# Both score passes of an attention block contract over 128 rows

## The chip, the cores and the metric

The kernel runs on one core of one Trainium2 chip. The metric is the time of one execution on the device in microseconds (us), the median of several executions; lower is better. TensorE (PE) does the matrix products, with its weight loads shown as a row of their own (PEld); VectorE (DVE), ScalarE (ACT) and GpSimd (POOL) do the elementwise work; DMAs are issued from the queue of SyncE (SP).

## The reference

Inputs are q, k and v of 8 batches, 8 heads, 576 tokens and 64 features, and a feed-forward with weights 512 x 2048 and 2048 x 512 whose activation is a quotient of polynomials. In short:

```python
scores = scale * np.matmul(q, k.transpose(0, 1, 3, 2))     # scale = 1/sqrt(64)
mask = block_i >= block_j                                  # blocks of 64 tokens
scores = np.where(mask, scores, -1000000000.0)
attn = softmax(scores)                                     # over the keys
x = (attn @ v) as [4608 tokens, 512 features]
h = x @ w_in
g = (a[0] + a[1]*h + a[2]*h2 + a[3]*h3) / (1 + |b[0]|*|h| + |b[1]|*h2 + 1e-6)
out = g @ w_out                                            # float32
```

## The kernel before

Every operand of a product is held as two numbers, a high part that the matrix engine multiplies exactly and a low remainder, and a product is the sum of the parts that matter: hi·hi, hi·lo and lo·hi.

**Attention.** Work goes by pairs of heads, 32 pairs in all. For a pair, `prep` transposes q and k so that features lie on the partitions (head 0 on rows 0 to 63, head 1 on rows 64 to 127), and splits them: ACT writes the high part (L357), DVE the remainder (L358). q hi, q lo and k hi go into the tile `hl`, k lo into a tile `kl`. Then two DMAs for each head build the tile `kq` (L365, L366): its first slot has q hi on the head's own 64 partitions and q lo on the other 64, its second slot has k hi on both halves. Three `kq` buffers serve the two heads of a pair and the first head of the next one.

`scores` takes the queries of a head in five blocks (t = 0 to 4; 64, 128, 128, 128 and 128 queries, against 64, 192, 320, 448 and 576 keys; the last in two pieces of 288). That makes 12 pieces for a pair and 384 in all. A piece has two passes into one bank of PSUM: L412 contracts over 128 rows (q hi and q lo with k hi), L413 over the head's own 64 rows (q hi with k lo, read from `kl`). Where the piece ends in the diagonal block (256 of the 384), a third matmul in bf16 adds the mask (L416). DVE takes the maximum of the bank (L417), ACT the exponential (L429), POOL multiplies by the reciprocal of the sum (L438, L442).

`transp` transposes the probabilities on PE (L463) and splits them into `pt1` (queries 0 to 319) or `pt2` (320 to 575), high part by ACT (L466), remainder by DVE (L467). Block 0 of the keys is the first 64 keys of both heads, side by side. `pv` multiplies with v, which lies in `vpad` between columns of zeros so that both heads of a pair come out of one product (L479), and stores x to DRAM (L484).

**Feed-forward.** It runs in two phases over d_ff: phase A (10 of 16 blocks) is woven into the attention from its second batch on, phase B follows alone. A unit of work is two blocks of d_ff for 256 tokens: `first` (24 matmuls, L201), the activation on ACT, POOL and DVE, `split` (L233, L234), and `second` (12 matmuls, L250). During the first batches DVE, ACT and POOL also split the float64 weights (L121 to L148).

**What sets the order.** The program emits attention step by step with lags: exponentials one step after the scores, transposes some ten steps after; feed-forward steps by a schedule in step numbers. The framework then reorders the instructions with its own model of time and fixes the order on each engine; at run time each engine takes its instructions in that order, and a waiting DMA on the SP queue holds those behind it.

Of the kernel before, what the change touches and what calls it, by code (L numbers as in the profile page):

```python
# [9 lines left out]
F32 = mybir.dt.float32  # L10
F32R = mybir.dt.float32r
# [12 lines left out]
CT = 256                 # tokens of a feed-forward chunk  # L24
# [35 lines left out]
def attn_ffn_kernel(  # L60
# [21 lines left out]
    # x^T, hi and lo (row = feature of a pair of heads) and the partial outputs  # L82
# [31 lines left out]
    def split_weights(pool, f0, nf, dt):  # L114
        wih, wil, woh, wol = weight_tiles(pool, f0, nf, dt)

        def place(dhi, dlo, src, nm):
            # float64 bits -> hi + lo
# [16 lines left out]
            # lo: the next 32 bits as a number, times the power of two, rounded to nearest  # L135
# [31 lines left out]
    class Ffn:  # L167
        def __init__(self):
            self.w = {}
            self.pools, self.hpools = [ffn], [ps_h]  # L170
            self.x, self.g, self.m = {}, {}, {}
            self.o = None
            self.n = 0
            self.ready = 0       # chunks whose tokens are there
# [124 lines left out]
    with ExitStack() as actx:  # L299
# [3 lines left out]
        pt1 = [apers.tile([128, 5, 320], F32R, name=f"pt1{x}") for x in "hl"]  # L303
        pt2 = [apers.tile([128, 9, 256], F32R, name=f"pt2{x}") for x in "hl"]
        vpad = [apers.tile([128, 9, 128], F32R, name=f"vp{x}") for x in "hl"]
        for x in pt1:
            nc.vector.memset(x[:, 3:5, 64:192].bitcast(F32), 0.0)
# [5 lines left out]
        # visits of pairs of heads: of the first batch all queries under 320 come first  # L313
# [27 lines left out]
        def prep(p, which):  # L341
            # rows: features of head 0, features of head 1; q hi, q lo, k hi
            s = st_[p]
            if which == 0:
                s["hl"] = att.tile([128, 3, S], F32R, name=f"hl{p}", tag="hl", bufs=1)
                s["kl"] = att.tile([128, S], F32R, name=f"kl{p}", tag="kl", bufs=2)
            raw, sc = (s["qr"], s["kr"])[which], (QSCALE, 1.0)[which]
            hl = s["hl"]
            h, l = (hl[:, 0], hl[:, 1]) if which == 0 else (hl[:, 2], s["kl"])
# [10 lines left out]
            if which == 1:  # L360
                # of a head: [q hi; q lo], [k hi; k hi], and for the odd head the halves change places
                for j in range(2):
                    kq = att.tile([128, 2, S], F32R, name=f"kq{p}_{j}", tag="kq", bufs=KQB)
                    src = hl[64 * j:64 * j + 64].bitcast(F32)
                    nc.sync.dma_start(out=kq[64 * j:64 * j + 64].bitcast(F32), in_=src[:, 0:3:2])  # L365
                    nc.sync.dma_start(out=kq[64 - 64 * j:128 - 64 * j].bitcast(F32), in_=src[:, 1:3])  # L366
                    s["kq", j] = kq

        def vprep(p):
            vr = st_[p]["vr"]  # L370
            vh, vl = vpad
            regs = [(slice(0, 64), slice(0, 1), slice(0, 64)), (slice(64, 128), slice(0, 1), slice(64, 128)),
                    (slice(0, 128), slice(1, 9, 2), slice(0, 64)), (slice(0, 128), slice(2, 9, 2), slice(64, 128))]
            for pr, bl, cl in regs:
                nc.scalar.copy(out=vh[pr, bl, cl], in_=vr[pr, bl, :])
                nc.gpsimd.tensor_tensor(out=vl[pr, bl, cl], in0=vr[pr, bl, :], in1=vh[pr, bl, cl].bitcast(F32),
                                        op=ALU.subtract)
# [3 lines left out]
        def bank(p, name):  # L381
            # the feed-forward's banks are free during the first batch
# [10 lines left out]
        def scores(p, t, j):  # L393
            s = st_[p]
            nq = NQ[t]
            if j == 0:
                pt = att.tile([128, 2, NK[t]], F32, name=f"p{p}_{t}", tag=f"p{t}", bufs=1)
                # block 0 of both heads, side by side
# [7 lines left out]
            rows = slice(64 * j, 64 * j + 64)  # L406
            banks = []
            for i, (c0, w) in enumerate(pieces(t)):
# [4 lines left out]
                nc.tensor.matmul(ps[:, :ww], lhsT=kq[rows, 0, qs], rhs=s["kl"][rows, c0:c0 + ww],  # L413
# [32 lines left out]
        def transp(p, t):  # L446
            pt, pk, _, _ = st_[p].pop(t)
            nq = NQ[t]
            hi, lo = pt1 if t < 3 else pt2
            c0 = Q0[t] if t < 3 else Q0[t] - 320  # L450
            nb = 1 + 2 * t
            groups = {1: [1], 3: [3], 5: [3, 2], 7: [4, 3], 9: [3, 3, 3]}[nb]
            blk = 0
            for gi, gn in enumerate(groups):
# [9 lines left out]
                dh = hi[:, blk:blk + gn, c0:c0 + nq]  # L464
                dl = lo[:, blk:blk + gn, c0:c0 + nq]
# [4 lines left out]
        def pv(p, g):  # L470
            b, hp = divmod(visits[p][0], NPAIR)
            hi, lo = (pt1, pt2)[g]
# [3 lines left out]
            for x in range(nb):  # L476
                s0 = 64 if (g == 0 and x > 0) else 0
                for i, (vv, pp) in enumerate(((vh, lo), (vh, hi), (vl, hi))):
                    nc.tensor.matmul(o[:, s0:w], lhsT=vv[:, x, :], rhs=pp[:, x, s0:w],  # L479
# [8 lines left out]
        # distance to the next use of an item's tiles  # L488
# [3 lines left out]
        def attn_steps():  # L492
            todo = []        # (step, function, arguments)
# [42 lines left out]
        done = 0          # feed-forward steps emitted  # L536
# [8 lines left out]
        KB = NPAIR * 10                          # attention steps of a batch  # L545
# [64 lines left out]
```

## Time and profile before

| | |
|---|---|
| time, median of 3 runs | 1444.44 us (1443.09 to 1444.92) |
| span of the profiled execution, first to last instruction | 1441.5 us |
| PE busy | 1405.4 us (97%), 8736 matmuls |
| DVE, ACT, POOL busy | 1025.7, 915.7, 957.1 us (71%, 64%, 66%) |
| last score piece starts | 1021.8 us into the span |
| DMA | 182.05 MB, mean 126 GB/s |

A matmul's time in the profile runs from its start to its end, and matmuls overlap in the array: the sum of the busy time is not the pace. The pace is read from one start to the next in a timeline. The idle time that a group shows is that of its engine just before it. The profile gives no time for the execution outside of its span.

### The profile page before, as it was taken

How to read it: one execution, taken by the hardware profiler on the slowest of the kernel's cores; microseconds unless marked ns; L12 is line 12 of the kernel's file. 1: busy time of each engine (PE TensorE's matmuls, PEld its weight loads, DVE VectorE, ACT ScalarE, POOL GpSimd, SP SyncE). 2: the span in 40 equal slices, each digit the busy share in tenths (PEclk: the TensorE clock that was granted, in tenths of full speed). 3: DMA queues.
4: the chain of work that ended last, by engine and by line, in shares of the span. 5: the costliest groups of instructions: out<-in, count | busy, mean ns of one | idle time of the engine just before them, and what ended most of it. 6: DMA issues, size and time to landing. Idle time of an engine off the chain costs nothing.

```text
span 1441.5 us, 25593 instructions
## 1 busy us (share of the span) xinstructions
PE 1405.4 (97%) x8736; PEld 1187.4 (82%) x8736; DVE 1025.7 (71%) x2016; ACT 915.7 (64%) x2218; POOL 957.1 (66%) x1240
## 2 busy tenths in 40 slices
PE   6999999999999999999999999999999999999998
PEld 4667788888888888888888888888989899999987
DVE  5887887776777777767666767666567777776765
ACT  4776677666666676766756756666555655555553
POOL 4888876766777766777666656657456766565554
PEclk9986899999999999999999999999999999999999
DMA  8676544546445464544443434433261244443332
GB/s 198 159 207 159 153 122 131 129 126 178 119 119 133 119 166 119 135 119 119 127 111 89 123 96 101 104 99 93 77 223 55 74 130 132 134 131 118 117 118 88
DMA packets 224610, 182.05 MB, mean 126 GB/s; under 512 B 131040, under 2 KB 194528, under 8 KB 224480
## 3 DMA queue, kind: packets, MB, share of 16 engines
q1 hardware_dynamic: 224416, 180.40, 46.0%
q8 instruction: 70, 1.15, 0.3%
q14 instruction: 60, 0.49, 0.1%
q0 software_dynamic: 64, 0.00, 0.0%
HBM read 98.57 MB, written 44.04 MB: 99 GB/s over the span
## 4 chain that ended last, share of the span: by engine, by line
PE 86%; DVE 5%; ACT 3%; DMA 3%; POOL 2%; issue 1%; SPq 0%; DVEq 0%; ACTq 0%; POOLq 0%
PE h L201 26%; PE o L250 24%; PE o L479 12%; PE s L413 8%; PE t L463 6%; PE s L412 5%; PE s L416 2%; PE tp L353 2%; POOL gl L234 1%; DVE u L224 1%; DMA x<-xscr 1%; DMA kq<-hl 1%; POOL u L211 1%; POOL v L210 1%; DVE v L225 0%
## 5 line engine op out<-in xcount | busy, mean ns | idle before, releaser
L201 PE MATMUL h<-x,wih 128*128 128x256 f32 x2304 | 441.9, 288 | 1.7 <-DVE s L213 0.9
L201 PEld LDWEIGHTS h<-x,wih 128*128 128x128 f32 x2304 | 368.0, 192 | 15.0 <-PE t L463 1.1
L201 PE MATMUL h<-x,wil 128*128 128x256 f32 x1152 | 329.1, 286 | 0.0
L417 DVE TENSOR_REDUCE nm<-s 128x1 f32<-128x288 f32 (+4 forms) x384 | 164.4, 430 | 160.5 <-PE s L416 83.6
L250 PE MATMUL o<-woh,gl 128*128 128x512 f32 x576 | 232.7, 404 | 3.4 <-POOL gl L234 2.7
L250 PE MATMUL o<-woh,gh 128*128 128x512 f32 x576 | 227.8, 396 | 0.0
L234 POOL TENSOR_TENSOR gl<-s,gh 128x512 fp32r<-128x512 f32 x144 | 190.3, 1322 | 56.4 <-ACT gh L233 51.7
L210 POOL TENSOR_SCALAR v<-u,bab 128x512 f32<-128x512 f32 x144 | 119.7, 831 | 162.5 <-ACT u L208 161.6
L250 PE MATMUL o<-wol,gh 128*128 128x512 f32 x576 | 227.2, 394 | 0.0
L429 ACT ACTIVATE p<-s,nm 128x288 f32<-128x288 f32 (+4 forms) x384 | 184.9, 485 | 62.6 <-DVE nm L417 46.7
L201 PEld LDWEIGHTS h<-x,wil 128*128 128x128 f32 x1152 | 220.6, 192 | 1.4
L442 POOL TENSOR_SCALAR p<-p,rc 128x128 f32<-128x128 f32 (+3 forms) x256 | 174.4, 693 | 41.3 <-DVE rc L437 34.7
L211 POOL TENSOR_TENSOR u<-v,u 128x512 f32<-128x512 f32 x144 | 190.4, 1322 | 8.6
L413 PE MATMUL s<-kl,kq 64*128 64x256 f32 (+3 forms) x384 | 162.6, 423 | 0.0
L208 ACT ACTIVATE u<-h 128x512 f32<-128x512 f32 x144 | 86.1, 598 | 118.4 <-PE h L201 116.1
L218 ACT ACTIVATE v<-u,qcb 128x512 f32<-128x512 f32 x144 | 104.6, 726 | 82.5 <-POOL u L211 82.1
L212 DVE TENSOR_TENSOR s<-s,h 128x512 f32<-128x512 f32 x144 | 98.4, 683 | 76.3 <-ACT s L209 75.7
L412 PE MATMUL s<-kq 128*128 128x256 f32 (+3 forms) x384 | 141.6, 369 | 8.4 <-DMA kq<-hl 5.9
L413 PEld LDWEIGHTS s<-kl,kq 64*128 64x128 f32 x384 | 73.6, 192 | 68.6 <-issue 41.5
L250 PEld LDWEIGHTS o<-woh,gl 128*128 128x128 f32 x576 | 109.1, 189 | 23.6 <-POOL gl L234 4.3
L250 PEld LDWEIGHTS o<-wol,gh 128*128 128x128 f32 x576 | 108.5, 188 | 23.0
L250 PEld LDWEIGHTS o<-woh,gh 128*128 128x128 f32 x576 | 109.2, 190 | 15.9
(98 smaller groups left out, 3002.8 us busy)
## 6 DMA issues: line engine op xcount, KB each, us to landing
kq<-hl SPq DMA_DIRECT2D x128, 288.0 KB, 4.2
x<-xscr SPq DMA_DIRECT2D x96, 256.0 KB, 3.6
xscr<-x SPq DMA_DIRECT2D x32, 320.0 KB, 4.7
qr<-in_q_dram SPq DMA_DIRECT2D x64, 144.0 KB, 2.7
kr<-in_k_dram SPq DMA_DIRECT2D x64, 144.0 KB, 2.6
pscr<-os SPq DMA_DIRECT2D x18, 512.0 KB, 2.7
pt<-pscr SPq DMA_DIRECT2D x18, 512.0 KB, 4.5
out_dram<-os SPq DMA_DIRECT2D x18, 512.0 KB, 3.3
```

The lines of the kernel that those rows point to most:

```text
L201: nc.tensor.matmul(h[:, j, :], lhsT=w[:, dc, fs], rhs=xs[dc // 2][:, dc % 2, hl, :], start=(dc == 0 and i == 0), stop=(dc == 3 and i == 2))
L210: nc.gpsimd.tensor_scalar(out=vt, in0=ut, scalar1=b1, scalar2=b0, op0=ALU.mult, op1=ALU.add)
L211: nc.gpsimd.tensor_tensor(out=ut, in0=vt, in1=ut, op=ALU.mult)
L218: nc.scalar.activation(out=vt, in_=ut, func=AF.Ln, bias=qcb)
L234: nc.gpsimd.tensor_tensor(out=gl.rearrange("p j t -> p (j t)"), in0=st, in1=gh.rearrange("p j t -> p (j t)").bitcast(F32), op=ALU.subtract)
L250: nc.tensor.matmul(self.o[m], lhsT=g[:, j, ms], rhs=w[:, f, :], start=(u == 0 and j == 0 and i == 0), stop=(u == nu - 1 and j == 1 and i = ...
L412: nc.tensor.matmul(ps[:, :ww], lhsT=kq[:, 0, qs], rhs=kq[:, 1, c0:c0 + ww], start=True, stop=False)
L413: nc.tensor.matmul(ps[:, :ww], lhsT=kq[rows, 0, qs], rhs=s["kl"][rows, c0:c0 + ww], start=False, stop=not last)
L417: nc.vector.reduce_max(out=nm[:nq, j, i:i + 1], in_=ps[:nq, :w], axis=AX.X, negate=True)
L429: nc.scalar.activation(out=pt[:nq, j, c0:c0 + w], in_=banks[i][:nq, :w], func=AF.Exp, bias=nm[:nq, j, 0:1], scale=1.0, accum_out=sm[:nq, j ...
L442: nc.gpsimd.tensor_scalar(out=pt[:nq, jj, 64:n], in0=pt[:nq, jj, 64:n], scalar1=rc[:nq, jj:jj + 1], scalar2=1.0, op0=ALU.mult, op1=ALU.mult)
L479: nc.tensor.matmul(o[:, s0:w], lhsT=vv[:, x, :], rhs=pp[:, x, s0:w], start=(x == 0 and i == 0), stop=(x == nb - 1 and i == 2))
```

## The change

The second score pass contracts over 128 rows too. `kl` is gone: `hl` has four slots (q hi, k hi, k lo, q lo), and `kq` has three: q hi on the head's own half and q lo on the other, k hi on both, k lo on both. Both passes now take the same stationary operand, `kq[:, 0]`, and the second pass adds q lo · k lo, which was left out before. Three DMAs for each head fill `kq` instead of two: the head's own half takes three slots in one DMA, the other half takes k hi and k lo in one, and q lo in one of its own.

Two more edits go with it. The zeros between the columns of v are shared by neighbouring blocks: `vpad` is 128 + 4·192 = 896 columns wide where it was 9·128 = 1152. And block 0 of P^T has a tile of its own, `pt0`, so the transposes of queries 0 to 319 go in groups of one block and the rest (1+2 and 1+4) where they went 3 and 3+2.

```diff
-            nc.vector.memset(x[:, 3:5, 64:192].bitcast(F32), 0.0)
+        pt0 = [apers.tile([128, 1, 320], F32R, name=f"pt0{x}") for x in "hl"]
+        pt1 = [apers.tile([128, 4, 256], F32R, name=f"pt1{x}") for x in "hl"]
+        vpad = [apers.tile([128, 128 + 4 * 192], F32R, name=f"vp{x}") for x in "hl"]
+            nc.vector.memset(x[:, 2:4, 0:128].bitcast(F32), 0.0)
...
-                s["hl"] = att.tile([128, 3, S], F32R, name=f"hl{p}", tag="hl", bufs=1)
-                s["kl"] = att.tile([128, S], F32R, name=f"kl{p}", tag="kl", bufs=2)
+                s["hl"] = att.tile([128, 4, S], F32R, name=f"hl{p}", tag="hl", bufs=1)
...
-            h, l = (hl[:, 0], hl[:, 1]) if which == 0 else (hl[:, 2], s["kl"])
+            h, l = (hl[:, 0], hl[:, 3]) if which == 0 else (hl[:, 1], hl[:, 2])
...
-                    kq = att.tile([128, 2, S], F32R, name=f"kq{p}_{j}", tag="kq", bufs=KQB)
+                    kq = att.tile([128, 3, S], F32R, name=f"kq{p}_{j}", tag="kq", bufs=KQB)
                     src = hl[64 * j:64 * j + 64].bitcast(F32)
-                    nc.sync.dma_start(out=kq[64 * j:64 * j + 64].bitcast(F32), in_=src[:, 0:3:2])
-                    nc.sync.dma_start(out=kq[64 - 64 * j:128 - 64 * j].bitcast(F32), in_=src[:, 1:3])
+                    other = kq[64 - 64 * j:128 - 64 * j].bitcast(F32)
+                    nc.sync.dma_start(out=kq[64 * j:64 * j + 64].bitcast(F32), in_=src[:, 0:3])
+                    nc.sync.dma_start(out=other[:, 1:3], in_=src[:, 1:3])
+                    nc.sync.dma_start(out=other[:, 0], in_=src[:, 3])
...
-                nc.tensor.matmul(ps[:, :ww], lhsT=kq[rows, 0, qs], rhs=s["kl"][rows, c0:c0 + ww],
+                nc.tensor.matmul(ps[:, :ww], lhsT=kq[:, 0, qs], rhs=kq[:, 2, c0:c0 + ww],
                                  start=False, stop=not last)
...
-            groups = {1: [1], 3: [3], 5: [3, 2], 7: [4, 3], 9: [3, 3, 3]}[nb]
+            groups = {1: [1], 3: [1, 2], 5: [1, 4], 7: [4, 3], 9: [3, 3, 3]}[nb]
...
-                    nc.tensor.matmul(o[:, s0:w], lhsT=vv[:, x, :], rhs=pp[:, x, s0:w],
+                    nc.tensor.matmul(o[:, s0:w], lhsT=vblock(vv, x), rhs=pp,
```

The framework orders the changed program anew, so instructions move on every engine. Lines of the changed file are 2 to 10 higher: L421, L422 and L425 are the former L412, L413 and L416; L369 to L371 the DMAs of `kq`; L470, L475 and L476 the transposes of the probabilities and their two splits.

PE, the scores of pair 14, query block 3 (`s14_3_0_0` and `s14_3_1_0` are the banks of its two heads; `h`, `o0` and `t13` belong to the feed-forward and to the pair before). Before:

```order
L412 MATMUL s14_3_0_0_5543<-kq14_0_5037 128x448
L413 MATMUL s14_3_0_0_5543<-kl14_4921,kq14_0_5037 128x448
L416 LDWEIGHTS mrow_104
L416 MATMUL s14_3_0_0_5543<-mcol_105,mrow_104 128x64
L412 MATMUL s14_3_1_0_5566<-kq14_1_5040 128x448
L413 MATMUL s14_3_1_0_5566<-kl14_4921,kq14_1_5040 128x448
L416 LDWEIGHTS mrow_104
L416 MATMUL s14_3_1_0_5566<-mcol_105,mrow_104 128x64
```

Now:

```order
L421 MATMUL s14_3_0_0_5603<-kq14_0_5091 128x448
L422 MATMUL s14_3_0_0_5603<-kq14_0_5091 128x448
L425 LDWEIGHTS mrow_104
L425 MATMUL s14_3_0_0_5603<-mcol_105,mrow_104 128x64
L201 MATMUL h0_5_0_6486<-x0_5_1_6303,wil0_143 128x256
L201 MATMUL h0_5_0_6486<-x0_5_1_6303,wih0_142 128x256 x2
L201 MATMUL h0_5_0_6486<-x0_5_1_6303,wil0_143 128x256
L250 MATMUL o0_4_0_6263<-woh0_144,gl0_4_3_6483 128x512
L421 MATMUL s14_3_1_0_5626<-kq14_1_5095 128x448
L422 MATMUL s14_3_1_0_5626<-kq14_1_5095 128x448
L425 LDWEIGHTS mrow_104
L425 MATMUL s14_3_1_0_5626<-mcol_105,mrow_104 128x64
```

The three matmuls of a piece still stand together, the second now reads `kq` alone, and other feed-forward matmuls stand between the two heads here.

SP, the DMAs that build `kq` of pair 15, with what stands between and behind them (`x` loads of the feed-forward, `xscr` stores of the attention). Before:

```order
L365 DMA kq15_0_5507<-hl15_5345 64x2x576
L366 DMA kq15_0_5507<-hl15_5345 64x1152
L484 DMA xscr3_76<-x13_0_5491 128x2x320
L185 DMA x0_5_1_6236<-xscr2_75 128x2x256 x2
L185 DMA x0_6_0_7073<-xscr2_75 128x2x192 x2
L185 DMA x0_6_0_7073<-xscr3_76 128x2x64 x2
L365 DMA kq15_1_5510<-hl15_5345 64x2x576
L366 DMA kq15_1_5510<-hl15_5345 64x1152
```

Now:

```order
L371 DMA kq15_0_5565<-hl15_5404 64x576
L185 DMA x0_5_1_6303<-xscr2_75 128x2x256 x2
L185 DMA x0_6_0_7145<-xscr2_75 128x2x192 x2
L335 DMA qr16_5773<-in_q_dram 96x6x64 x2
L185 DMA x0_6_0_7145<-xscr3_76 128x2x64
L369 DMA kq15_0_5565<-hl15_5404 64x1728
L370 DMA kq15_0_5565<-hl15_5404 64x1152
L494 DMA xscr3_76<-x13_0_5549 128x2x320
L185 DMA x0_6_0_7145<-xscr3_76 128x2x64
L369 DMA kq15_1_5569<-hl15_5404 64x1728
L370 DMA kq15_1_5569<-hl15_5404 64x1152
L371 DMA kq15_1_5569<-hl15_5404 64x576
```

For the first head q lo goes ahead, before k is there, and two DMAs follow; for the second head all three stand in a row.

ACT, the copies of the transposed probabilities of pair 14, query block 1 (`t14_1`). Before:

```order
L209 ACTIVATE s0_5_0_6445<-h0_5_0_6418,ncoef_113 128x512
L128 ACTIVATE wao10_2_6499<-sto10_2_6497 128x512
L466 CAST pt1h_128<-t14_1_0_5753 128x3x128
L140 ACTIVATE wpo10_2_6501<-wpo10_2_6501 128x512
L429 ACTIVATE p15_0_5724,sm15_0_5726<-s15_0_1_0_5749,nm15_0_5725 64x64
```

Now:

```order
L475 CAST pt0h_128<-t14_0_0_5760 128x64
L438 ACTIVATE p15_0_5784,sm15_0_5786<-s15_0_0_0_5787,nm15_0_5785 64x64
L475 CAST pt0h_128<-t14_1_0_5813 128x128
L438 ACTIVATE p15_0_5784,sm15_0_5786<-s15_0_1_0_5809,nm15_0_5785 64x64
L475 CAST pt1h_130<-t14_1_1_5817 128x2x128
```

One copy of three blocks has become one of a single block and one of two, into two tiles and out of two banks.

More of the change, by code (lines that the diff above doesn't have):

```diff
@@ L301, in attn_ffn_kernel @@
         apers = actx.enter_context(tc.tile_pool(name="apers", bufs=1))
-        pt1 = [apers.tile([128, 5, 320], F32R, name=f"pt1{x}") for x in "hl"]
+        pt0 = [apers.tile([128, 1, 320], F32R, name=f"pt0{x}") for x in "hl"]
+        pt1 = [apers.tile([128, 4, 256], F32R, name=f"pt1{x}") for x in "hl"]
         pt2 = [apers.tile([128, 9, 256], F32R, name=f"pt2{x}") for x in "hl"]
-        vpad = [apers.tile([128, 9, 128], F32R, name=f"vp{x}") for x in "hl"]
+        vpad = [apers.tile([128, 128 + 4 * 192], F32R, name=f"vp{x}") for x in "hl"]
         for x in pt1:
-            nc.vector.memset(x[:, 3:5, 64:192].bitcast(F32), 0.0)
+            nc.vector.memset(x[:, 2:4, 0:128].bitcast(F32), 0.0)
         for x in pt2:
@@ L370, in vprep, with vblock @@
             vr = st_[p]["vr"]
[L371 to L377, printed above, removed]
+            at = [lambda x: x[0:64, 0:64].unsqueeze(1), lambda x: x[64:128, 64:128].unsqueeze(1),
+                  lambda x: x[:, 128:].rearrange("p (b c) -> p b c", c=192)[:, :, 0:64],
+                  lambda x: x[:, 128:].rearrange("p (b c) -> p b c", c=192)[:, :, 128:192]]
+            of = [vr[0:64, 0:1], vr[64:128, 0:1], vr[:, 1:9:2], vr[:, 2:9:2]]
+            for f, src in zip(at, of):
+                vh, vl = (f(x) for x in vpad)
+                nc.scalar.copy(out=vh, in_=src)
+                nc.gpsimd.tensor_tensor(out=vl, in0=src, in1=vh.bitcast(F32), op=ALU.subtract)
+        def vblock(x, b):
+            c = 0 if b == 0 else 128 + 192 * ((b - 1) // 2) + 64 * ((b - 1) % 2)
+            return x[:, c:c + 128]
         nbank = [0]
@@ L405, in scores @@
             qs = slice(Q0[t], Q0[t] + 128)
-            rows = slice(64 * j, 64 * j + 64)
             banks = []
@@ L448, in transp @@
             nq = NQ[t]
-            hi, lo = pt1 if t < 3 else pt2
-            c0 = Q0[t] if t < 3 else Q0[t] - 320
             nb = 1 + 2 * t
-            groups = {1: [1], 3: [3], 5: [3, 2], 7: [4, 3], 9: [3, 3, 3]}[nb]
+            groups = {1: [1], 3: [1, 2], 5: [1, 4], 7: [4, 3], 9: [3, 3, 3]}[nb]
             blk = 0
@@ L463, in transp @@
                     nc.tensor.transpose(ps[:, i, :nq], src, ident[:nq, :nq])
-                dh = hi[:, blk:blk + gn, c0:c0 + nq]
-                dl = lo[:, blk:blk + gn, c0:c0 + nq]
+                (hi, lo), b0, c0 = ((pt2, blk, Q0[t] - 320) if t > 2 else (pt0, 0, Q0[t]) if blk == 0 else
+                                    (pt1, blk - 1, Q0[t] - 64))
+                dh = hi[:, b0:b0 + gn, c0:c0 + nq]
+                dl = lo[:, b0:b0 + gn, c0:c0 + nq]
                 nc.scalar.copy(out=dh, in_=ps[:, :gn, :nq])
@@ L471, in pv @@
             b, hp = divmod(visits[p][0], NPAIR)
-            hi, lo = (pt1, pt2)[g]
             vh, vl = vpad
@@ L477, in pv @@
                 s0 = 64 if (g == 0 and x > 0) else 0
+                hi, lo = ((y[:, x] for y in pt2) if g else (y[:, 0] for y in pt0) if x == 0 else
+                          (y[:, x - 1] for y in pt1))
                 for i, (vv, pp) in enumerate(((vh, lo), (vh, hi), (vl, hi))):
-                    nc.tensor.matmul(o[:, s0:w], lhsT=vv[:, x, :], rhs=pp[:, x, s0:w],
+                    nc.tensor.matmul(o[:, s0:w], lhsT=vblock(vv, x), rhs=pp,
                                      start=(x == 0 and i == 0), stop=(x == nb - 1 and i == 2))
```

## The prediction

> **What bounds the kernel now.** I read the engines' totals first, then the engines by stage, then PE's timeline around one score piece.
>
> ```profile
> PE 1405.4 (97%) x8736; PEld 1187.4 (82%) x8736; DVE 1025.7 (71%) x2016; ACT 915.7 (64%) x2218; POOL 957.1 (66%) x1240
> PE 86%; DVE 5%; ACT 3%; DMA 3%; POOL 2%; issue 1%; SPq 0%; DVEq 0%; ACTq 0%; POOLq 0%
> ```
>
> PE is busy 97% of the span, and 86% of the chain that ended last lies on it. Where that holds is in the table by stage (columns: stretch, length, then busy time of PE, PEld, DVE, ACT and POOL, granted clock, DMA share, GB/s).
>
> ```profile
> 40.00:160.00 120.00, 109.53 (x561) 85.38 (x561) 100.96 (x239) 84.80 (x245) 104.44 (x142) 0.80 0.71 185
> 400.00:650.00 250.00, 247.67 (x1596) 206.49 (x1595) 182.54 (x392) 170.98 (x454) 174.57 (x248) 1.00 0.50 131
> 1025.00:1441.00 416.00, 407.88 (x2599) 369.21 (x2597) 285.23 (x398) 224.55 (x369) 244.22 (x216) 1.00 0.38 120
> ```
>
> Three stages: up to about 160 us the attention runs without much feed-forward, DVE (84%) and POOL (87%) are nearly full and PE has gaps and a granted clock of 0.80. From there to 1025 us attention and feed-forward are woven together, PE idles 2.3 of 250 us, the others stand at 73%, 68% and 70%. From 1025 us phase B runs alone; it has no scores and does not change. Since PE is full in the middle stage, the next question is whether its matmuls run at their pace. This is PE just before the attention ends (start, length):
>
> ```profile
> 1020.68 0.28 PE L479 MATMUL o<-pt2h,vph 128*128 128x256 f32 x1
> 1020.80 0.28 PE L479 MATMUL o<-pt2h,vpl 128*128 128x256 f32 x1
> 1020.92 0.29 PE L412 MATMUL s<-kq 128*128 128x288 f32 x1
> 1021.14 0.40 PE L413 MATMUL s<-kl,kq 64*128 64x288 f32 x1
> 1021.47 0.40 PE L412 MATMUL s<-kq 128*128 128x288 f32 x1
> 1021.80 0.40 PE L413 MATMUL s<-kl,kq 64*128 64x288 f32 x1
> 1022.13 0.20 PE L416 MATMUL s<-mcol,mrow 128*128 128x64 bf16 x1
> 1022.17 0.48 PE L250 MATMUL o<-woh,gl 128*128 128x512 f32 x1
> 1022.49 0.40 PE L250 MATMUL o<-woh,gh 128*128 128x512 f32 x1
> 1022.72 0.40 PE L250 MATMUL o<-wol,gh 128*128 128x512 f32 x1
> 1023.05 0.27 PE L463 MATMUL t<-ident,p 64*128 64x64 f32 x1
> 1023.25 0.50 PE L250 MATMUL o<-woh,gl 128*128 128x512 f32 x1
> ```
>
> Read the starts. 256 columns at full rows take 0.12 us (1020.68 to 1020.80), 512 take 0.23 (1022.49 to 1022.72), so 288 should take about 0.134. From L412 to L413 it is 0.22, from L413 to the next matmul 0.33: the 64-row pass costs 0.09 before and 0.20 behind itself, and no wait is shown. It is not the score data: the only other matmul with 64 rows, the transpose L463, shows the same, since its 64 columns take 0.20 where the mask's 64 columns at 128 rows take 0.04. The row form is what these two share.
>
> **The change part by part.**
>
> *The second pass at full rows.* In the middle stage, two rows count the pieces, and how many have a mask:
>
> ```profile
> L413 PE MATMUL s<-kl,kq x314: 379/395/579, 160.8 to 1021.8; 64*128 64x288 f32 x53, 64*128 64x256 f32 x52, 64*128 64x320 f32 x26, 64*128 64x448 f32 x26
> L416 PE MATMUL s<-mcol,mrow x209: 202/203/233, 161.8 to 1022.1; 128*128 128x64 bf16 x105
> ```
>
> With the pace 0.12 for 256 columns and 0.23 for 512 between them, both masked and unmasked pieces read like the one above: 0.28 to 0.29 us over the pace from L412 to the matmul behind the piece. Without a mask that next matmul is late as well (1021.47 to 1021.80, 0.33 where 0.22 would do): 0.38 in all. With a mask it is the L250 at 1022.17, 0.32 instead of 0.23; but there the short mask matmul leaves little cover for the next weight load in any case, so I count nothing (if it goes, 209 x 0.08 = 17 us more). Freed on PE: 105 x 0.38 + 209 x 0.285 = 39.9 + 59.6 = 99.5 us. The pace of the new L422 is that of L479, since rows, types and columns are alike.
>
> A rule in the Trainium skill speaks against a full saving. TensorE: Matmul & The Clock Gate, Part 3, says that a weight load overlaps running matmuls only where the row groups differ. The rows:
>
> ```profile
> 1020.68 0.19 PEld L479 LDWEIGHTS o<-pt2h,vpl 128*128 128x128 f32 x1
> 1021.14 0.18 PEld L413 LDWEIGHTS s<-kl,kq 64*128 64x128 f32 x1
> ```
>
> The full-row load for the matmul at 1020.80 starts at 1020.68 with a full-row matmul in flight: it overlaps, while the 64-row load starts only with its own matmul. By the rule L422's load would stay exposed like L413's; what that gives is a rival below.
>
> *What of the 99.5 us arrives.* The middle stage would shrink from 865 us to 765, by 0.885, and the others' shares rise from 73, 68 and 70% to 82, 77 and 79%. From below, nothing is given back: DVE, ACT and POOL have room. From above, the stage 40 to 160 us shows what fuller engines do: at DVE 84% PE idles 10.5 of 120 us (8.7%), at 73% it idles 0.9%; on the line between them 82% means about 7.5% of 765 us, less the 0.9% it idles already, 50 us back. That stage lacks feed-forward matmuls to fill PE's gaps, and the middle stage has them, so I take a value nearer to the lower end: 20 us.
>
> *A third DMA for each `kq`.* They are on the path only where the buffer comes late. The second head's buffer is the one that the first head of the pair before frees:
>
> ```profile
> 412.40 0.20 PE L416 MATMUL s<-mcol,mrow 128*128 128x64 bf16 x1
> 412.50 0.62 SPq L365 DMA_DIRECT2D kq<-hl  x1
> 413.17 0.60 SPq L366 DMA_DIRECT2D kq<-hl  x1
> 423.66 0.28 PE L412 MATMUL s<-kq 128*128 128x256 f32 x1
> L365 SPq DMA_DIRECT2D kq<-hl x64: 616/641/1399, 8.8 to 984.7; - x64
> DMA to landing us min/median/max: 3.2/4.2/8.6
> ```
>
> The last reader ends about 412.5, the DMAs go out at once, the first use is at 423.66: 11.2 us, times 0.885 is 9.9. Three issues of 0.64 and a landing of 4.2 us make 6.1, with the longest landing 10.5. Half as many bytes again can lengthen the landing. I take 0.1 us for each of 26 pairs, 3 us; from below 0, from above the longest landing each time, 0.6 x 26 = 16 us. Behind these DMAs on SP wait an `xscr` store and feed-forward `x` loads, which the 0.64 us delays; `x` is asked for a unit ahead. The first head's q lo goes out early, so its two late DMAs are as before.
>
> *Up to 160 us.* 384 - 314 = 70 pieces give 70 x 0.32 / 0.85 = 26 us on PE, of which I count 8, since DVE and POOL set that stage. The `kq` DMAs are on the chain there:
>
> ```profile
> 11.29 6.76 DMA kq<-hl
> 50.18 5.07 DMA kq<-hl
> ```
>
> A third issue, and a first one that now waits for k lo too (one DVE pass of 0.45 us, by its row below), cost about 1.3 us in each of three pairs: 4 us. Net 4 us gained; bounds 26 gained and 4 lost.
>
> *Split groups.* For block 1 one copy of three blocks becomes one and two.
>
> ```profile
> L466 ACT CAST pt1h<-t 128x384 fp32r<-128x384 f32 x64 | 30.5, 476 | 32.4 <-PE t L463 32.1
> L466 ACT CAST pt1h<-t 128x256 fp32r<-128x256 f32 x32 | 12.1, 379 | 2.5 <-PE t L463 2.4
> L466 ACT CAST pt1h<-t 128x64 fp32r<-128x64 f32 x32 | 6.8, 213 | 11.0 <-PE t L463 10.9
> L467 DVE TENSOR_TENSOR pt1l<-t,pt1h 128x384 fp32r<-128x384 f32 x64 | 35.1, 549 | 5.2 <-ACT pt1h L466 5.1
> L467 DVE TENSOR_TENSOR pt1l<-t,pt1h 128x256 fp32r<-128x256 f32 x32 | 13.2, 412 | 0.9 <-ACT pt1h L466 0.9
> L358 DVE SCALAR_TENSOR_TENSOR kl<-tp,hl 128x288 fp32r<-128x288 f32 x64 | 27.9, 448 | 4.1 <-ACT hl L357 3.8
> ```
>
> 128 columns lie a third of the way from 64 (213 ns) to 256 (379): some 268 ns. So ACT gains 32 x (268 + 379 - 476) = 5.5 us, and DVE, with about the same 270, 32 x (270 + 412 - 549) = 4.3. Block 2 (1+4 for 3+2) comes out even. Both lie beside PE's work and are in the 20 us; without that cover they would cost 5.5 us. 32 more banks are taken, one a pair, from the ring that scores share; no row prices that alone, and it too is in the 20. The shared zeros keep counts and sizes of ACT's and POOL's work on v, and shorten two memsets at the start: nothing.
>
> *The mask behind a full-row pass.* The bf16 load of 96 ns now follows a full-row fp32 matmul, which no row shows. In the other direction, mask to L250, the next start comes after 0.04 us. I take nothing; from above 256 x 0.096 = 25 us.
>
> **Sum.** 1441.5 - 99.5 + 20 + 3 - 4 = 1361.0 us of span. The median of the runs lies 1444.4 - 1441.5 = 2.9 us above it: 1364 us.
>
> **The rivals.**
>
> *A. Nothing is given back.* For it: the transposes stand far behind their scores in the order, so latency matters little. Against: DVE above 80%. 1364 - 23 - 18 (the rest of the first stage) = 1323, and with the matmul behind the mask 1306.
>
> *B. DVE, ACT and POOL take the bound.* 50 us given back, or the mask's load exposed for 25 us with 45 given back: 1364 + 30 to 1364 + 50, about 1404. For it: all three would stand near 80%, in fixed orders that depend on each other. Against: buffers are many and PE has feed-forward to do meanwhile.
>
> *C. The first gap stays.* 384 x 0.09 = 35 us are missing, of which 80% (as of the 99.5) would have arrived, 28 us: 1392. It is what the rule on weight loads quoted above would give; the PEld rows of L479 speak against it, and I leave it 3 in 100.
>
> *D. The change doesn't do what it says.* The gaps belong to two passes over one bank, and stay at any row count: no gain, and some 1445 us with the added DMAs. L479 and L250 write one bank many times at pace, and L463 shows the gap with no second pass. Of the Trainium skill this would be the statement in TensorE: Matmul & The Clock Gate, "Why this matters for your kernels", that a matmul with few rows takes the same time as one with 128; the row of L413 shows that it does not where the forms alternate.
>
> *E. Slower: `kq` arrives too late.* The second head's first score heads PE's queue, so everything behind it stops. The freed time of a pair is 99.5 / 26 = 3.8 us, about 3.1 after what is given back; the wait exceeds it once the DMAs land later than 9.9 + 3.1 = 13 us after the release. At 14 us each pair loses 1 us: 1444 + 26 = 1470. Against it: 6.1 us expected, 10.5 at the longest.
>
> **How the numbers follow.** The forecast 0.64, A 0.13, B 0.14, C 0.03, D 0.03, E 0.03. The forecast's own range is 1342 to 1388 (10 to 40 us given back, the DMA and mask bounds in part). Over the cases, 8 in 10 need A's 1323 and B's 1404 about: 1322 to 1402. A measurement of this kernel tells about 0.2% (3 us) from no change. Faster by more: forecast, A, B and C, 0.94; less 0.01 where B goes to its end, 0.93. Same: half of D, 0.02. Slower: E and the rest of D, 0.05.
>
> **What the profile will show.** L422's rows at 128 rows with 0.134 us from start to start at 288 columns and no idle time of "issue" on PEld before it; L412's successor likewise. The last score near 941 us instead of 1022, phase B again some 416 us. DVE, ACT and POOL at 80 to 82, 76 and 78% in the middle stage, PE idle there 2 to 4%. The wait for `kq` at most a few us outside the first batch. Wrong would be: L421 to L422 still over 0.2 us at 288 columns (C or D), PE idle over 6% in the middle with waits for DVE or ACT (B), or many waits for `kq` (E).

## The result

The changed kernel takes 1392.44 us (median; 1389.48 to 1395.31), the kernel before 1443.76 us in the same comparison: a ratio of 0.9639, 95% interval 0.9606 to 0.9672, about 51 us less. The forecast was 1364 us, in a range of 1322 to 1402. The direction and the mechanism came out; the gain was 51 us instead of 80. The forecast's own range, 1342 to 1388, does not hold 1392; the whole range does.

The page of the kernel after, with the totals of the engines and the chain that ended last, and then the longest of PE's waits (us in total, times, longest).

```profile
span 1387.7 us, 25820 instructions
PE 1294.4 (93%) x8736; PEld 1165.6 (84%) x8736; DVE 1029.0 (74%) x2048; ACT 909.7 (66%) x2250; POOL 955.3 (69%) x1240
PE 72%; DVE 9%; DMA 6%; POOL 5%; ACT 4%; issue 2%; SPq 1%; DVEq 0%; POOLq 0%; ACTq 0%
```

```profile
PE s L421 <- DMA kq<-hl: 11.2, 4, 4.7
PE h L201 <- DMA x<-xscr: 7.9, 5, 2.6
PE o L489 <- DVE pt0l L476: 7.0, 5, 2.0
PE o L250 <- POOL gl L234: 6.8, 7, 2.0
```

PE's busy time fell by 111 us and its share of the last chain from 86% to 72%; the rest went to waits of many kinds, none of them large. The stages, in the same columns as before:

```profile
0.00:40.00 40.00, 17.04 (x81) 12.80 (x81) 23.38 (x63) 20.31 (x57) 20.26 (x36) 0.91 0.99 211
40.00:160.00 120.00, 90.39 (x538) 77.41 (x537) 105.19 (x238) 83.45 (x245) 104.52 (x136) 0.81 0.74 198
160.00:400.00 240.00, 227.16 (x1601) 206.26 (x1600) 187.19 (x411) 171.33 (x473) 181.67 (x257) 0.97 0.63 159
400.00:650.00 250.00, 237.60 (x1684) 213.90 (x1684) 197.78 (x424) 176.45 (x484) 182.21 (x262) 0.99 0.62 157
650.00:900.00 250.00, 246.89 (x1779) 224.47 (x1778) 185.61 (x412) 183.64 (x494) 178.59 (x266) 1.00 0.57 139
```

In the middle stage PE idles 12.8 + 12.4 + 3.1 = 28 us, where it idled 4 us before in the same stretches. From 40 to 160 us it does less in the same time: 90 us busy of 120, and 538 matmuls where the kernel before made 561.

PE's timeline of the kernel after, one masked piece in the middle and one at the end, with the weight loads of the latter:

```profile
702.12 0.31 PE L421 MATMUL s<-kq 128*128 128x320 f32 x1
702.27 0.31 PE L422 MATMUL s<-kq 128*128 128x320 f32 x1
702.42 0.20 PE L425 MATMUL s<-mcol,mrow 128*128 128x64 bf16 x1
702.46 0.48 PE L250 MATMUL o<-woh,gl 128*128 128x512 f32 x1
702.77 0.40 PE L250 MATMUL o<-woh,gh 128*128 128x512 f32 x1
...
961.08 0.29 PE L421 MATMUL s<-kq 128*128 128x288 f32 x1
961.22 0.29 PE L422 MATMUL s<-kq 128*128 128x288 f32 x1
961.35 0.20 PE L425 MATMUL s<-mcol,mrow 128*128 128x64 bf16 x1
```

```profile
960.97 0.19 PEld L421 LDWEIGHTS s<-kq 128*128 128x128 f32 x1
961.09 0.19 PEld L422 LDWEIGHTS s<-kq 128*128 128x128 f32 x1
```

Both gaps are gone: 288 columns take 0.14 and 0.13 us where they took 0.22 and 0.33, 320 take 0.15 each. The weight load of L422 starts 0.13 us ahead of its matmul, under L421. The mask's bf16 load costs nothing that shows behind a full-row pass (0.13 from L422 to the mask), and the matmul behind the mask is as late as before (702.46 to 702.77, 0.31 for 512 columns).

Where the 54 us of span went shows in when the pieces start. A pair has 12 pieces, so the 73rd start of the first pass begins pair 6 and the 373rd the last pair. The rows of that line, cut off at these points (first and last start), of the kernel before and after:

```profile
L412 PE MATMUL s<-kq x73: 279/442/740, 16.2 to 162.1; 128*128 128x256 f32 x25, 128*128 128x288 f32 x24, 128*128 128x320 f32 x12, 128*128 128x448 f32 x12
L412 PE MATMUL s<-kq x373: 276/364/740, 16.2 to 990.7; 128*128 128x256 f32 x63, 128*128 128x288 f32 x62, 128*128 128x320 f32 x31, 128*128 128x448 f32 x31
```

```profile
L421 PE MATMUL s<-kq x73: 274/402/722, 17.1 to 169.5; 128*128 128x256 f32 x25, 128*128 128x288 f32 x24, 128*128 128x320 f32 x12, 128*128 128x448 f32 x12
L421 PE MATMUL s<-kq x373: 274/364/722, 17.1 to 935.1; 128*128 128x256 f32 x63, 128*128 128x288 f32 x62, 128*128 128x320 f32 x31, 128*128 128x448 f32 x31
```

| | before | after | change |
|---|---|---|---|
| up to pair 6 | 162.1 | 169.5 | +7.4 |
| pair 6 to pair 31 | 828.6 | 765.6 | -63.0 |
| from pair 31 to the end | 450.8 | 452.6 | +1.8 |

So the gain lies where it was expected. The first stage, counted as 4 us of gain, lost 7. The stretches do not hold quite the same work: up to pair 6 the change has issued 60 feed-forward matmuls (`first` and `second`), the kernel before 46, and in the middle 2478 against 2496. At 0.12 us for one of `first` and 0.23 for one of `second`, up to 3 of the 7 us are feed-forward that was moved ahead (an estimate).

### The profile page after: what moved, and what is told of

Same layout as the page of the kernel before. It is cut to its first block, busy times and chain, and to the rows that moved or that the text cites. A ratio compares the mean times of both kernels' runs of the same rounds, so it can differ in the third digit from the quotient of the medians.

```text
span 1387.7 us, 25820 instructions
## 1 busy us (share of the span) xinstructions
PE 1294.4 (93%) x8736; PEld 1165.6 (84%) x8736; DVE 1029.0 (74%) x2048; ACT 909.7 (66%) x2250; POOL 955.3 (69%) x1240
## 4 chain that ended last, share of the span: by engine, by line
PE 72%; DVE 9%; DMA 6%; POOL 5%; ACT 4%; issue 2%; SPq 1%; DVEq 0%; POOLq 0%; ACTq 0%
PE h L201 26%; PE o L250 25%; PE o L489 9%; PE t L470 4%; PE s L421 3%; PE s L422 3%; PE tp L355 2%; DMA x<-xscr 2%; DMA kq<-hl 2%; DVE nm L426 1%; ACT p L438 1%; POOL gl L234 1%; DVE v L225 1%; DVE u L224 1%; DMA xscr<-x 1%
## 5 line engine op out<-in xcount | busy, mean ns | idle before, releaser
L201 PEld LDWEIGHTS h<-x,wih 128*128 128x128 f32 x2304 | 372.3, 194 | 21.6 <-issue 7.6
L426 DVE TENSOR_REDUCE nm<-s 128x1 f32<-128x288 f32 (+4 forms) x384 | 161.4, 427 | 84.8 <-PE s L425 49.9
L451 POOL TENSOR_SCALAR p<-p,rc 128x128 f32<-128x128 f32 (+3 forms) x256 | 165.0, 656 | 31.6 <-DVE rc L446 29.3
L421 PE MATMUL s<-kq 128*128 128x256 f32 (+3 forms) x384 | 136.3, 357 | 24.0 <-DMA kq<-hl 11.2
L250 PEld LDWEIGHTS o<-wol,gh 128*128 128x128 f32 x576 | 108.7, 189 | 22.4
L470 PE MATMUL t<-ident,p 128*128 128x128 f32 (+1 forms) x672 | 113.0, 279 | 7.2 <-POOL p L451 2.3
L422 PE MATMUL s<-kq 128*128 128x256 f32 (+3 forms) x384 | 119.0, 312 | 0.0
```

The lines of the kernel that those rows point to most:

```text
L201: nc.tensor.matmul(h[:, j, :], lhsT=w[:, dc, fs], rhs=xs[dc // 2][:, dc % 2, hl, :], start=(dc == 0 and i == 0), stop=(dc == 3 and i == 2))
L250: nc.tensor.matmul(self.o[m], lhsT=g[:, j, ms], rhs=w[:, f, :], start=(u == 0 and j == 0 and i == 0), stop=(u == nu - 1 and j == 1 and i = ...
L421: nc.tensor.matmul(ps[:, :ww], lhsT=kq[:, 0, qs], rhs=kq[:, 1, c0:c0 + ww], start=True, stop=False)
L422: nc.tensor.matmul(ps[:, :ww], lhsT=kq[:, 0, qs], rhs=kq[:, 2, c0:c0 + ww], start=False, stop=not last)
L426: nc.vector.reduce_max(out=nm[:nq, j, i:i + 1], in_=ps[:nq, :w], axis=AX.X, negate=True)
L451: nc.gpsimd.tensor_scalar(out=pt[:nq, jj, 64:n], in0=pt[:nq, jj, 64:n], scalar1=rc[:nq, jj:jj + 1], scalar2=1.0, op0=ALU.mult, op1=ALU.mult)
```

## The experiments

Each time below is a median, with the ratio to the kernel before measured beside it and its 95% interval. "First" is the start of pair 6, "middle" the time from there to pair 31; both are read from the one run that was profiled, which can lie several us off the median.

| kernel | time, us | ratio | first | middle |
|---|---|---|---|---|
| before | 1444 | | 162.1 | 828.6 |
| the change with a 64-row second pass | 1486.65 | 1.0278 (1.0248 to 1.0307) | 187.1 | 842.7 |
| before with the split groups | 1460.28 | 1.0113 (1.0081 to 1.0145) | 173.9 | 830.9 |
| flat tile, 64-row second pass | 1470.18 | 1.0182 (1.0161 to 1.0204) | 178.5 | 839.0 |
| before, weights' split left out | 1444.75 | 1.0003 (0.9984 to 1.0021) | 154.9 | 842.1 |
| the change | 1392.44 | 0.9639 (0.9606 to 0.9672) | 169.5 | 765.6 |
| flat tile | 1397.55 | 0.9681 (0.9659 to 0.9703) | 170.8 | 769.7 |
| one bank | 1387.16 | 0.9615 (0.9593 to 0.9637) | 169.7 | 751.7 |
| fixed buffers, two DMAs | 1528.34 | 1.0573 (1.0541 to 1.0605) | 206.4 | 877.0 |
| zero half, two DMAs | 1392.99 | 0.9653 (0.9630 to 0.9676) | 168.5 | 781.2 |
| the change, weights' split left out | 1372.22 | 0.9516 (0.9488 to 0.9544) | 155.1 | 763.6 |
| the change without its second pass | 1375.29 | 0.9515 (0.9478 to 0.9551) | 174.0 | 750.4 |
| the change, less DVE in phase A | 1379.85 | 0.9560 (0.9542 to 0.9578) | 175.1 | 763.6 |
| one bank, chunks ready later | 1404.98 | 0.9739 (0.9713 to 0.9765) | 167.0 | 767.4 |

### Back to 64 rows, all else kept

```diff
-                nc.tensor.matmul(ps[:, :ww], lhsT=kq[:, 0, qs], rhs=kq[:, 2, c0:c0 + ww],
+                nc.tensor.matmul(ps[:, :ww], lhsT=kq[64 * j:64 * j + 64, 0, qs], rhs=kq[64 * j:64 * j + 64, 2, c0:c0 + ww],
```

> The changed kernel, with the second pass contracting over the head's own 64 rows again (q hi with k lo, read from the third slot of kq); the three DMAs, the shared zeros and the split groups stay. Theory (the 64-row form costs PE 0.28 to 0.38 us a piece, some 120 us in all, and the added DMAs cost the first stage some 10 us): the gaps of 0.09 before and 0.20 behind the second pass come back, and the time goes to 1445 to 1465 us, at or above the kernel before. Rival (the gain came from the new order of the instructions, or from reading kq in place of kl): it stays within 10 us of 1392.

It took 1486.65 us, above the range: 94 us more than the change, and 41 us more than the kernel before. Its rows, the 73rd and 373rd start and one piece:

```profile
L421 PE MATMUL s<-kq x73: 279/415/740, 17.1 to 187.1; 128*128 128x256 f32 x25, 128*128 128x288 f32 x24, 128*128 128x320 f32 x12, 128*128 128x448 f32 x12
L421 PE MATMUL s<-kq x373: 276/364/740, 17.1 to 1029.8; 128*128 128x256 f32 x63, 128*128 128x288 f32 x62, 128*128 128x320 f32 x31, 128*128 128x448 f32 x31
```

```profile
1058.68 0.29 PE L421 MATMUL s<-kq 128*128 128x288 f32 x1
1058.91 0.40 PE L422 MATMUL s<-kq 64*128 64x288 f32 x1
1059.23 0.20 PE L425 MATMUL s<-mcol,mrow 128*128 128x64 bf16 x1
```

With the rows the gaps come back, 0.23 and 0.32 us for 288 columns, with the same operand tile, bank and number of passes. So they are of the row form, and the rival that the gain came from a new order or from `kq` in place of `kl` falls. It also tells that the rest of the change, in the order laid for it, costs 41 us beside a 64-row pass, 25 of them up to pair 6 and 14 in the middle. Of the 25, some 8 are feed-forward done earlier (102 of its matmuls up to pair 6, where the kernel before has 46; an estimate as above), and they are missing in the middle.

### What the rest of the change costs

The split groups with the shared zeros, on the kernel before (the edits of `pt0`, `pt1`, `vpad`, `vblock` and `groups` from the diff):

> The kernel before, with the shared zeros, pt0 and the split groups (1+2, 1+4) alone. Theory (32 more copies on ACT and DVE, 5.5 and 4.3 us, lie beside PE's work): 1444, within 4 us. Rival (the added bank and copies a pair hold PE up, and are a part of what was given back): 1452 or more.

1460.28 us, 15 more than before: the rival. In the profiled run, whose span is 13.5 us longer, 11.8 of them are lost up to pair 6:

```profile
L418 PE MATMUL s<-kq x73: 280/446/740, 16.3 to 173.9; 128*128 128x256 f32 x25, 128*128 128x288 f32 x24, 128*128 128x320 f32 x12, 128*128 128x448 f32 x12
```

The third DMA and the shared zeros alone, with a 64-row pass. The split is undone by a flat tile: queries 64 on of block b lie at column 256 b + q, so that one copy reaches all blocks.

```diff
+        pt1 = [apers.tile([128, 64 + 5 * 256], F32R, name=f"pt1{x}") for x in "hl"]
...
+                    dh, dl = (y[:, 64:].rearrange("p (b c) -> p b c", c=256)[:, blk:blk + gn, Q0[t] - 64:Q0[t] - 64 + nq]
+                              for y in pt1)
```

> The flat tile and the unsplit groups, with the second pass over the head's own 64 rows: of the change only the third DMA with its traffic and the shared zeros are left. Theory (the third DMA costs what is left of the 41 us by which the changed kernel with a 64-row second pass is behind, after 15 for the split groups): 1444 + 26 = 1470, between 1462 and 1478, all of it lost by pair 12. Rival (the DMA costs a few us as predicted, the rest is order): under 1455.

1470.18 us, some 26 more than before, as the theory said; but by the starts 16 are lost up to pair 6 and 10 behind it. Beside 64-row passes the prices add up, 15 and 26 make the 41, though the shared zeros are in both and the flat tile is an edit of its own. The same flat tile with the full-row pass:

> The changed kernel with pt0 and pt1 as one flat tile of 64 + 5 x 256 columns (block b of query q lies at column 256 b + q), of the same size in memory; the transposes go in groups of 3 and 3+2 again, with one copy each. Theory (the split groups cost what the run of them alone showed, 15 us): 1372 to 1384. Rival (that price was of the order that the framework happened to make there): 1386 to 1398.

1397.55 us: no gain over the change. So the 15 us of the split groups do not come back beside a full-row pass, as the rival had it, by which that price belongs to the order laid there and not to the groups (what the flat tile itself costs was not tried). That run and the one before differ in the row form alone, 73 us, with 2480 and 2483 feed-forward matmuls in the middle. One bank for the three transposes of block 1, with two copies out of it:

```diff
-            groups = {1: [1], 3: [1, 2], 5: [1, 4], 7: [4, 3], 9: [3, 3, 3]}[nb]
+            groups = {1: [1], 3: [3], 5: [1, 4], 7: [4, 3], 9: [3, 3, 3]}[nb]
...
+                for k0, kn in ([(0, 1), (1, 2)] if (t == 1) else [(0, gn)]):
```

> The changed kernel, with the three transposes of query block 1 in one bank again; two copies on ACT and two on DVE take them out of it (block 0 to pt0, the rest to pt1). The split groups alone cost the kernel before 15 us. Theory (the added bank of PSUM a pair is what they cost): 1376 to 1384. Rival (the added copies, or pt0 as a tile of its own, are what they cost): 1388 to 1396.

1387.16 us lies between the two expectations, and its interval overlaps that of the change. Inconclusive: the medians differ by 5 us. The short middle, 751.7 us, is no gain: 124 feed-forward matmuls fewer fall into it than in the change (2354 against 2478), some 20 us by the estimate above, and from pair 31 to the end it takes 467 us where the change takes 453.

Two DMAs a head instead of three, first with `kq` in three fixed buffers:

```diff
+        kqs = [apers.tile([128, 3, S], F32R, name=f"kq{x}") for x in range(KQB)]
...
+                    nc.sync.dma_start(out=kq[64 * j:64 * j + 64].bitcast(F32), in_=src[:, 1:4])
+                    nc.sync.dma_start(out=other[:, 0:2], in_=src[:, 0:3:2])
```

> The changed kernel with two DMAs for each head instead of three and 737 KB instead of 885 KB a head: hl holds q lo, q hi, k hi, k lo, kq stays in three fixed buffers, and k lo goes to the head's own half alone. The other half of the third slot keeps what the buffer held before (zeros, then the k lo of an earlier head), so that the term q lo times k lo is not the right one; it is of the size of the term that the kernel before left out. Theory (the added kq traffic holds up the first stage): pair 6 starts at 155 to 163 us instead of 169.5, the time is 1375 to 1385. Rival (the first stage is held up by DVE and POOL alone, the middle stage by the engines): 1392, within 4 us.

1528.34 us (1.0573, 1.0541 to 1.0605), far from both. PE's longest wait is the reason that nothing follows from it for the traffic:

```profile
PE s L423 <- DMA kq<-hl: 80.2, 19, 9.9
```

With the fixed buffers `kq` came late 19 times, which says nothing of the number of DMAs. A second way keeps the two-slot `kq` of before and lets DVE write k lo into halves of zero-padded tiles:

```diff
+                for rs, l_ in ([(slice(0, 128), l)] if which == 0 else
+                               [(slice(64 * j, 64 * j + 64), klz[p % 2][j]) for j in range(2)]):
...
+                nc.tensor.matmul(ps[:, :ww], lhsT=kq[:, 0, qs], rhs=klz[p % 2][j][:, c0:c0 + ww],
```

> The flat tile, and a second pass over 128 rows without a third DMA: kq has two slots and two DMAs as before the change, and DVE writes k lo of each head into a tile of its own whose other half is zero (two tiles a head, in turn), as the moving operand of the second pass. DVE makes four passes for a pair where it made two, 0.45 us each, 29 us more in all. Theory (the third DMA is what holds up the first stage, some 20 us): 1355 to 1368, pair 6 before 162 us. Rival (DVE sets the first stage, and is near its bound in the middle): 1380 or more.

1392.99 us, as the change, on the rival's side. The traffic did what it should, by the landings up to 165 us (DMAs, KB each, median us), first the kernel before, then the change, then this one:

```profile
kq<-hl SPq DMA_DIRECT2D x28, 288.0 KB, 4.9
```

```profile
kq<-hl SPq DMA_DIRECT2D x13, 432.0 KB, 6.2
kq<-hl SPq DMA_DIRECT2D x13, 288.0 KB, 6.1
kq<-hl SPq DMA_DIRECT2D x13, 144.0 KB, 5.0
```

```profile
kq<-hl SPq DMA_DIRECT2D x28, 288.0 KB, 4.6
```

The 288 KB landings are longer in the change, 6.1 us where they were 4.9, and 4.6 without the added bytes. In the kernel before and in this one half of these DMAs are the first of a row, in the change none is; of the second in a row alone the medians are 5.1, 6.1 and 5.1 us. Yet pair 6 starts at 168.5 us instead of 169.5. DVE has 31 us more to do in this kernel (1060.3 against 1029.0), so the two may cancel; the price of the traffic beside full-row passes stays open. Its longer middle, 781.2 us, holds 54 feed-forward matmuls more than that of the change.

### What bounds PE now

The second pass taken out of the changed kernel:

```diff
-                nc.tensor.matmul(ps[:, :ww], lhsT=kq[:, 0, qs], rhs=kq[:, 2, c0:c0 + ww],
-                                 start=False, stop=not last)
```

> The changed kernel without its second score pass (q with k lo is left out; kq is filled as before). That takes 384 full-row matmuls, 55 us at pace, off PE (45 us of it in the middle stage) and nothing else. Theory that PE still sets the middle stage in full: 1345 to 1350. Theory that a part of each freed us is lost to waits, as with the change (63 of 99.5 us arrived): about 1364. Theory that DVE, ACT, POOL or the DMAs set the middle stage now: 1382 to 1392.

1375.29 us, between the second and the third expectation: of the 43 us that this takes off PE in the middle (300 matmuls at a pace of 0.143 us, an estimate), 15 arrive (766 to 750), 35%. Of the 95 us that the row form freed there (25 pairs of 3.8) the first comparison shows 77 (842.7 to 765.6) and the flat pair 69 (839.0 to 769.7), 73 to 81%. A part of what is missing in the 35% is the granted clock, in the same columns as before:

```profile
160.00:400.00 240.00, 219.11 (x1450) 194.22 (x1450) 187.20 (x408) 167.66 (x467) 180.84 (x255) 0.93 0.62 157
```

It is 0.93 here and 0.97 in the change in the same stretch. The profiled run took 1379.11 us at a mean clock of 0.961; another run of this kernel took 1370.58 at 0.973, the clock of the change's profiled run. If these 8.5 us all lay in the middle, 55% would arrive (an estimate). So PE's time has become worth less than it was; how much less lies between.

I took DVE for the engine that takes it back, and left out the two DVE passes of its correction step in phase A (L225 with the same condition):

```diff
+            if ph == 1:
+                nc.vector.scalar_tensor_tensor(out=ut, in0=ut, scalar=QC, in1=r0, op0=ALU.add, op1=ALU.mult)
```

> The changed kernel without the two DVE passes of the correction step of the reciprocal in phase A (L224, L225: the reciprocal stays as the exponential gives it): 90 x 1.5 us = 137 us less on DVE, some 105 of them between pair 6 and pair 31, and nothing else. Theory (DVE, at 78% in its fixed order, takes back a part of what PE was given): from pair 6 to 31 in 735 to 750 us instead of 766, time 1360 to 1378. Rival (PE still sets that stretch, or the transfers do): over 760 us, time over 1385.

The middle took 763.6 us where it took 765.6, though DVE's share there fell from 79% to 66% (of the kernel with less DVE):

```profile
400.00:650.00 250.00, 237.24 (x1677) 213.63 (x1677) 166.19 (x382) 178.37 (x487) 175.98 (x267) 0.98 0.62 156
```

PE is as busy as with DVE at 79%, and the middle holds the same feed-forward work (2476 matmuls against 2478). My theory falls: DVE's load is not what takes back the middle stage. The time, 1379.85 us, lies between the two expectations, but what is gained lies behind pair 31: the span is 1377.5 us, the last pair starts at 938.6, which leaves 439 us where there were 453. Last, the chunks of the feed-forward, whose loads of x PE waits for, asked for three steps later:

```diff
-        LAST = ALAG3 + 3
+        LAST = ALAG3 + 6
```

> The changed kernel with one bank for query block 1 (1387 us) whose feed-forward chunks count as ready six instead of three steps after the tenth (three attention steps, some 9 us, later). Theory (PE's waits for x, 7.9 us and the stores behind them on the chain, come from chunks that are asked for too early): 1372 to 1380, wait of the first feed-forward matmuls for x under 3 us. Rival (they are a small part, and a later start costs as much): 1384 to 1395.

1404.98 us, above both expectations and 18 more than the same kernel without the delay, and the wait remains:

```profile
PE h L201 <- DMA x<-xscr: 7.5, 5, 3.9
```

So that theory falls too. What holds PE for 28 us of the middle is left open; ACT, POOL and the ring of banks were not tried alone. PE's waits from 165 to 900 us name no single cause: 6.7 us for `x`, 8.9 for `pt0l`, which the change brought in, 4.7 for `gl`. In the kernel with the flat tile, which has no `pt0`, 12.0 us are for `pt1l`.

### The first stage

Of the weights' split of phase A, five DVE passes, one POOL and one ACT pass a piece left out, in both kernels:

```diff
+            if dt is F32R:
+                nc.scalar.activation(out=pt, in_=w0.bitcast(U32), func=AF.Copy, scale=2.0 ** -43)
...
+                return
```

> The kernel before, with the split of phase A's weights cut to one ACT conversion, one ACT copy and one POOL product a piece (five DVE passes, one POOL and one ACT pass a piece left out, so the weights of phase A are not the right ones): 20 pieces x 3.3 us = 65 us less on DVE and 31 us less on POOL in the first stage. Theory (DVE and POOL set the first stage, PE does not): pair 6 starts 30 to 45 us earlier than 162 us, at 117 to 132, where PE's own work with its 64-row gaps becomes the bound; time 1400 to 1415. Rival (the kq transfers or PE set it): pair 6 after 145.

> The changed kernel with the same cut. Theory (in the first stage the full-row form is worth nothing because DVE and POOL set it; with them out of the way it is worth up to the 26 us that PE saves there): pair 6 starts 10 to 25 us before that of the kernel before with the same cut, and the time is 70 to 90 us lower than that kernel's. Rival (the added kq traffic and the split groups hold up the first stage): pair 6 not earlier than there, and the time lower by 45 to 60 us only.

The 73rd start of the first pass and PE's wait for `kq`, first of the kernel before without that split, then of the changed kernel without it:

```profile
L418 PE MATMUL s<-kq x73: 279/397/740, 16.0 to 154.9; 128*128 128x256 f32 x25, 128*128 128x288 f32 x24, 128*128 128x320 f32 x12, 128*128 128x448 f32 x12
```

```profile
PE s L418 <- DMA kq<-hl: 12.1, 4, 4.5
```

```profile
L427 PE MATMUL s<-kq x73: 283/415/741, 18.4 to 155.1; 128*128 128x256 f32 x25, 128*128 128x288 f32 x24, 128*128 128x320 f32 x12, 128*128 128x448 f32 x12
```

```profile
PE s L427 <- DMA kq<-hl: 22.4, 7, 5.8
```

With 54 us less on DVE and 50 on POOL (by the totals of the two pages) the kernel before reaches pair 6 only 7 us earlier (the rival's side), and its whole time does not change (ratio 1.0003); the changed kernel gains 14 and arrives at the same 155. The stretch from 40 to 160 us, of the kernel before and of the changed kernel, both without the split:

```profile
40.00:160.00 120.00, 110.10 (x633) 86.49 (x633) 66.96 (x176) 86.31 (x256) 71.45 (x136) 0.91 0.71 187
40.00:160.00 120.00, 98.13 (x665) 87.87 (x665) 71.92 (x187) 89.70 (x269) 74.53 (x139) 0.88 0.84 216
```

In the kernel before DVE falls from 84% to 56% and POOL from 87% to 60%, and PE idles 9.9 us where it idled 10.5. So DVE and POOL set that stage in a small part, not as I thought. In the changed kernel PE waits 22.4 us for `kq` instead of 12.1, which speaks for the transfers. But the time fell by 72.5 us between the two, not by the 45 to 60 of that rival. So in that stage the change as a whole is worth nothing even with DVE and POOL out of the way: PE needs less, and what it waits for comes as late as before or later.

## Why the prediction was right, and where it was off

**The bound and the mechanism** were right. PE set the middle stage, and the gaps were of the 64-row form: 0.23 and 0.32 us for 288 columns with it, 0.14 and 0.13 without, with the same tile, bank and number of passes. The Trainium skill has a rule for it, in TensorEngine Tiling (Array Packing), Key Properties: changing the tiling mode drains TensorE. The trace agrees, with about 0.09 us ahead of the 64-row pass and 0.19 behind it. The rule of the Trainium skill that stood behind rival C (TensorE: Matmul & The Clock Gate, Part 3), that a weight load overlaps running matmuls only where the row groups differ, does not hold here: the load of L422 starts 0.13 us ahead of its matmul with the same rows. The mask's load was taken at nothing, and is nothing; the further 17 us behind the mask were rightly not counted.

**The middle stage** was sized about right: 99.5 us freed with 20 given back and 3 for `kq`, 76.5 net. Measured are 63 from before to after, and 69 to 77 where the row form alone differs: 18 to 26 us given back, and some 14 (842.7 against 828.6) that the other edits cost. But the reason given, fuller engines and DVE above all, was not confirmed: DVE's share cut by a sixth changed nothing. So the size of the 20 came out without its cause, in part by luck. Of the signs, PE idles 4% from 160 to 900 us and `kq` made it wait in the first 165 us alone, as forecast; DVE, ACT and POOL stand at 77, 72 and 73% there where 80 to 82, 76 and 78 were forecast, and the last score piece starts at 961 us, not 941.

**The step that failed** is "Up to 160 us", with "Split groups" beside it. It reckoned 8 us gained from the row form, because DVE and POOL set that stage, and 4 lost to the third DMA, net 4. (Its own terms for the latter, 0.64 and 0.45 us, make 1.1 us a pair and not 1.3.) The row form did free PE, which was busy 117 us up to pair 6 instead of 138, but PE idled 53 us there instead of 24. DVE and POOL set the stage in a small part at most, as the kernels without the weights' split show. Beside a 64-row pass the other edits cost 25 us up to pair 6 (187.1 against 162.1); with full rows 18 fewer, so 7 remain lost, 3 of which may be feed-forward moved ahead (the estimate above). The bounds of that term, 26 gained and 4 lost, hardly hold it.

I had put the split groups into the 20 us, or at 5.5 where nothing covers them; with the shared zeros they cost 15 beside a 64-row pass, 12 of them up to pair 6. Missing cover does not explain that: 6 of 32 pairs have some 2 us of the added copies (an estimate from the 5.5 and 4.3 of the prediction). Whether it is the bank or the order stays open. How the 7 divide stays open too: without the third DMA or without the split groups the full-row kernels reach pair 6 at 168.5 and 170.8, so neither alone is it. Nor does the chain of the first 165 us settle it: `kq`'s DMAs hold 7.2% of it in the kernel before, 13.2% in the change, and 4.5% in the full-row kernel with the flat tile, which is no faster.

**The rivals.** B's 1404 and C's 1392 are nearer to the time measured than the forecast, but neither mechanism is what happened: C's gap is gone, so its number is right by chance, and most of what B put down to full engines is in the first stage and in the other edits (11 and 14 of the 28 us above the forecast). That the range holds 1392 is owed to B's number at its upper end. A, D and E did not come about; `kq` cost PE 11.2 us of waits where it cost 5.9.

**What these runs can't settle.** Each edit has the framework lay a new order. The middle stage of the five kernels with a 64-row pass took 829 to 843 us. That of six full-row kernels took 764 to 781, whatever else differed; left out are the one without its second pass, the one with fixed buffers (877 us, held up by `kq`) and the one bank (752 us, some 771 with the feed-forward work that the change has there). The 68 us between the means of the two groups stand well clear of that spread; terms under some 15 us are not told apart by one build each.

No run beats the change clearly. The kernel with one bank has the lowest median of those that leave nothing out (0.9615 against 0.9639), with overlapping intervals.

## What to carry to other kernels

Read a matmul's cost from start to start, not from its busy time: here a 64-row matmul among full-row ones cost 0.3 us each time, and filling the idle rows with an operand that is there anyway was cheaper. Try the edits that make room for a change by themselves, in every stage: here they cost most in the first one, which the sum put at 4 us of gain. And do not trust the share of a busy engine to name the bound: DVE and POOL stood at 84 and 87% there, and cutting them moved little. Once an engine is freed, its next microsecond is worth less; here it went from 73 to 81% to something between 35 and 55%.

## What was not expected of the hardware

The landing of a 288 KB copy within SBUF, second in a row of DMAs, rose from 5.1 to 6.1 us in the first 165 us when half as many bytes again went into each `kq`; the core's DMA share rose from 0.70 to 0.80 there. From 165 to 900 us the same copies landed in 4.5 us at a share of 0.48 and in 5.3 at 0.60. That a copy waits for other copies fits these figures; how much of it is the larger copy just ahead in the row was not tried apart.
